# From the fourth group on, every engine works in written order: attention steps placed by hand among the feed-forward units, and the last weight blocks made inside that group

## The chip, the core and the metric

The kernel runs on one core of a Trainium2 chip. Its time is the device time of one execution in microseconds, as the median of repeated executions. Five engines work side by side, each through its own queue of instructions in order, and wait for one another through semaphores: TensorE (PE in the profile, its weight loads PEld), VectorE (DVE), ScalarE (ACT), GpSimd (POOL) and SyncE (SP, which here only issues DMAs). An instruction that waits holds up all that stands behind it on its engine, and nothing on the others, until they need its result.

## What is computed

Block attention over 8 batches, 8 heads and 576 positions in chunks of 64, and behind it a feed-forward layer with `h - tanh(h)` between its two matrices:

```python
scores = scale * np.matmul(q_c, k_c.transpose(0, 1, 2, 4, 3))   # 64 x 64 within a chunk
scores = scores - np.max(scores, axis=-1, keepdims=True)
attn = np.exp(scores)
attn = attn / (np.sum(attn, axis=-1, keepdims=True) + 1e-09)
out = np.matmul(attn, v_c)
x = out.transpose(0, 2, 1, 3).reshape(B * S, H * D)             # 4608 x 512
h = x @ w_in                                                    # w_in 512 x 2048
g = h - np.tanh(h)
return (g @ w_out).astype(np.float32)                           # w_out 2048 x 512
```

## The kernel before

**Groups.** The 4608 rows are worked through in nine groups of 512 (`SIZES`, four tiles of 128 rows). The attention of a group runs ahead of its feed-forward, in two halves `b` of two tiles each. Numbers are kept as a high and a low part (`xh`, `xl` and so on), and a product takes three matmul passes: high by high, high by low, low by high.

**The three first groups** (0 to 2) use `FeedForward`. In group 1 the first matrix is converted to half precision (`Half.convert`). In group 2 `Half.combine(j)` and `Half.shorten(j)`, for j = 0 to 7, make sums of blocks of the second matrix for a fast product: `combine` is six additions on POOL (L434 to L441), `shorten` four ACT scalings and four DVE subtractions (L454, L455) that leave `fast_w[j]`.

**From the fourth group on** (3 to 8, `FAST = 3`) `Fast` computes a product of the second matrix with seven instead of eight block products. A group has 16 units: (b, j), two halves of eight. For unit s, `Fast.run` issues:
- `gemm1(s)`: 24 matmuls on PE into `ph` (L576), of which there are two buffers;
- `shrink(s)`: tanh on ACT (L583), `ph - tanh` on DVE into u, which the profile calls `xl` (L584), and three sums on POOL (L585 to L587); u has two buffers;
- `split(s-1)`: high part on ACT (L596), low part on DVE (L597), of the unit before;
- `gemm2(s-3)`: 21 matmuls into `po` (L614), three units late. At the turn from one half to the next it pauses for one unit, so that two `gemm1` stand back to back and then two `gemm2`; `finish` (L629 to L640: 2 ACT, 6 DVE and 2 POOL instructions, 2 DMAs) empties `po` after unit 7 and unit 15.

**The attention of the next group** (`Late`) is laid between the units by `interleaved`: `sums` (largest values of q and k on ACT, L107, and of v on DVE, L124, then a maximum over partitions on POOL, L114, and small DVE instructions), `split` of q, k and v (ACT L297, DVE L298), `scores` (96 small matmuls, L308), `exponents`, `normalise`, `transpose` (to half precision, then two DMA transposes on SP, L348) and `values` (96 matmuls, then L360 and L361). `load` issues the DMAs of the group after that.

**What sets the order.** The text is only a wish: from the bar in `PLAN` on, a scheduler places instructions on every engine by the rank of their text and its own estimate of when operands are ready. So steps of a later group can be pulled ahead, on each engine by itself. What the scheduler has chosen is fixed before the kernel runs; on the chip each queue is worked in order.

Two things limit how far attention can be pulled apart: the tile `a` exists once and holds the split k, then the exponentials on their way to the DMA transposes, and, in this kernel, also the throwaway output of `sums` (L107); and `psa` in PSUM exists once for scores and values.

## Time and profile before

| What | us |
|---|---|
| median of 3 runs (lowest, highest) | 944.98 (944.39, 945.45) |
| the profiled execution's own time | 946.89 |
| its span, first to last instruction | 944.3 |
| busy in the span: PE, DVE, ACT, POOL | 849.3, 611.3, 473.3, 263.3 |

The mean granted TensorE clock of that execution was 0.965. In the trace, group 3 begins with its first `gemm1` at 339.76 us and group 8, the last, at 852.69. A row of the timeline reads: start, length, engine, line, operation, output<-inputs, shape, count, and in brackets how long the engine stood idle before it and what it waited for. "Busy" adds up instruction lengths; matmuls overlap their neighbours, so that a row of 24 matmuls is some 0.16 us longer than the step from its start to the start of the next row.

### The profile page before, as it was taken

The numbers are of one execution on the slowest core, as the hardware profiler recorded it, in microseconds if no ns is written. First come the engines' busy times: TensorE is split into PE (matmuls) and PEld (weight loads), VectorE is DVE, ScalarE is ACT, GpSimd is POOL, SyncE is SP. The second block draws the span as 40 slices with busy tenths as digits, with TensorE's granted clock in tenths as the row PEclk, the third lists the DMA queues.
The fourth block names the chain that finished last, engine by engine and source line by source line (L and its number), as shares of the span: only waits on it lengthen the run. The fifth ranks groups of instructions, "written<-read, shape, count | busy, mean of one in ns | idle before, by whom it ended". The sixth has DMA issues, their size and how long they took to land.

```text
span 944.3 us, 19977 instructions
## 1 busy us (share of the span) xinstructions
PE 849.3 (90%) x8525; PEld 700.0 (74%) x8525; DVE 611.3 (65%) x878; ACT 473.3 (50%) x767; POOL 263.3 (28%) x375
## 2 busy tenths in 40 slices
PE   9999999999998869897988888978979888889997
PEld 7888778887565558776876777767867777768886
DVE  6987987777787776465656466565746565555343
ACT  7797967656454744435434444336343534433342
POOL 0000000000266364242332242342323252334342
PEclk9999999999999969998999999999999899989999
DMA  9763534212220220303021122112131101010000
GB/s 257 220 192 138 175 100 140 52 46 70 88 51 19 26 108 24 69 24 90 24 68 47 24 68 68 46 40 74 47 49 43 24 24 24 12 36 24 1 23 23
DMA packets 61400, 63.14 MB, mean 67 GB/s; under 512 B 32640, under 2 KB 40832, under 8 KB 61312
## 3 DMA queue, kind: packets, MB, share of 16 engines
q1 hardware_dynamic: 61312, 61.88, 22.6%
q8 instruction: 66, 1.08, 0.5%
q14 instruction: 22, 0.18, 0.1%
HBM read 45.09 MB, written 9.44 MB: 58 GB/s over the span
## 4 chain that ended last, share of the span: by engine, by line
PE 32%; DVE 25%; POOL 14%; ACT 12%; issue 8%; DMA 7%; SPq 2%; ACTq 0%; DVEq 0%; POOLq 0%
PE ph L495 10%; PE po L519 9%; PE ph L576 6%; PE po L614 5%; POOL xl L587 4%; DVE xl L584 4%; DMA s<-a 4%; POOL xl L585 4%; ACT wh L596 4%; ACT gh L596 3%; DVE gl L597 3%; POOL xl L586 3%; DVE wh L597 2%; DVE wh L298 2%; DVE a L298 1%
## 5 line engine op out<-in xcount | busy, mean ns | idle before, releaser
L576 PE MATMUL ph<-xh,wl 128*128 128x256 f16 x2160 | 271.3, 286 | 45.5 <-DVE xl L584 45.3
L576 PEld LDWEIGHTS <-wl 128*128 128x128 f16 x2160 | 220.3, 102 | 84.1 <-issue 49.5
L585 POOL TENSOR_TENSOR xl<-xl 128x256 f32<-128x256 f32 x96 | 70.3, 733 | 357.0 <-DVE xl L584 293.2
L597 DVE SCALAR_TENSOR_TENSOR gl<-xl,to_g,gh 128x896 f16<-128x896 f32 x48 | 55.3, 1152 | 131.6 <-ACT gh L596 131.6
L596 ACT ACTIVATE gh<-xl,to_g 128x896 f16<-128x896 f32 x48 | 50.0, 1041 | 145.2 <-POOL xl L587 134.7
L597 DVE SCALAR_TENSOR_TENSOR wh<-xl,to_g,wh 128x896 f16<-128x896 f32 x48 | 59.1, 1231 | 80.3 <-ACT wh L596 80.2
L596 ACT ACTIVATE wh<-xl,to_g 128x896 f16<-128x896 f32 x48 | 50.0, 1042 | 119.7 <-POOL xl L587 119.7
L614 PEld LDWEIGHTS <-wh 128*128 128x128 f16 x1008 | 98.6, 98 | 11.4
L614 PE MATMUL po<-wl,wh 128*128 128x256 f16 x576 | 91.6, 273 | 0.0
L519 PE MATMUL po<-wh,gh 128*128 128x512 f32 x192 | 79.9, 416 | 4.4 <-ACT gh L510 4.4
L495 PE MATMUL ph<-xh,wl 128*128 128x512 f16 (+2 forms) x324 | 77.0, 375 | 4.0 <-DVE t L504 3.0
L614 PE MATMUL po<-wh,wh 128*128 128x256 f16 x432 | 78.5, 273 | 0.0
L519 PE MATMUL po<-wh,gl 128*128 128x512 f32 x192 | 76.5, 403 | 1.8 <-DVE gl L511 1.8
L519 PE MATMUL po<-wl,gh 128*128 128x512 f32 x192 | 76.4, 398 | 0.0
L584 DVE SCALAR_TENSOR_TENSOR xl<-ph,sig,t 128x512 f32<-128x512 f32 x96 | 71.0, 740 | 7.7 <-ACT t L583 7.7
L614 PEld LDWEIGHTS <-gh 128*128 128x128 f16 x672 | 65.7, 98 | 12.9 <-issue 4.9
L587 POOL TENSOR_TENSOR xl<-xl 128x256 f32<-128x256 f32 x96 | 71.4, 744 | 0.0
L583 ACT ACTIVATE t<-ph,sig 128x512 f32<-128x512 f32 x96 | 64.6, 673 | 3.9 <-PE ph L576 3.6
L614 PE MATMUL po<-wh,gh 128*128 128x256 f16 x336 | 55.7, 274 | 3.9 <-DVE wh L627 3.9
L308 PEld LDWEIGHTS <-wh 64*64 64x64 f16 x2688 | 27.4, 112 | 34.1 <-issue 33.7
L614 PE MATMUL po<-wl,gh 128*128 128x256 f16 x336 | 52.4, 273 | 0.0
L511 DVE TENSOR_TENSOR gl<-t,gh 128x512 fp32r<-128x512 f32 (+1 forms) x52 | 38.5, 742 | 19.5 <-ACT gh L510 17.4
(146 smaller groups left out, 1449.8 us busy)
## 6 DMA issues: line engine op xcount, KB each, us to landing
raw<-w_in SPq DMA_DIRECT2D x16, 512.0 KB, 3.9
raw<-w_out SPq DMA_DIRECT2D x16, 512.0 KB, 5.2
out<-wh SPq DMA_DIRECT2D x32, 256.0 KB, 2.0
rawk<-kL SPq DMA_DIRECT2D x28, 256.0 KB, 3.0
rawv<-vL SPq DMA_DIRECT2D x28, 256.0 KB, 2.9
xl<-qL SPq DMA_DIRECT2D x28, 256.0 KB, 2.8
qbd<-qE SPq DMA_DIRECT2D x16, 128.0 KB, 4.9
k<-kE SPq DMA_DIRECT2D x8, 256.0 KB, 5.0
```

The lines of the kernel that those rows point to most:

```text
L298: nc.vector.scalar_tensor_tensor(out=hl[1], in0=raw, scalar=to, in1=hl[0], op0=ALU.mult, op1=ALU.subtract)
L495: nc.tensor.matmul(ph, lhsT=self.weight(fc, 0, a)[:, kc * P:(kc + 1) * P], rhs=x[b][:, kc, cols], start=(k == 0), stop=(k == 3 * KC - 1))
L511: nc.vector.tensor_sub(gl, t, gh)
L519: nc.tensor.matmul(self.po[t], lhsT=gg[a][:, ts], rhs=self.weight(fc, 1, b), start=(fc == 0 and i == 0), stop=(fc == FC - 1 and i == 2))
L576: nc.tensor.matmul(self.ph[:, 1 - f::2, :], lhsT=half_w[fc][:, w, kc * P:(kc + 1) * P], rhs=rhs, start=(k == 0), stop=(k == 3 * KC - 1))
L583: nc.scalar.activation(t, self.ph, AF.Tanh, scale=sig)
L584: nc.vector.scalar_tensor_tensor(out=u[:, :4], in0=self.ph, scalar=sig, in1=t, op0=ALU.mult, op1=ALU.subtract)
L585: nc.gpsimd.tensor_add(u[:, 4:6], u[:, 1:3], u[:, 0:4:3])
L587: nc.gpsimd.tensor_sub(u[:, 0:4:3], u[:, 0:2], u[:, 2:4])
L596: nc.scalar.activation(gh, u, AF.Copy, scale=powers[1])
L597: nc.vector.scalar_tensor_tensor(out=gl, in0=u, scalar=powers[1], in1=gh, op0=ALU.mult, op1=ALU.subtract)
L614: nc.tensor.matmul(place[m], lhsT=part[:, self.SUM[m]], rhs=w[m][:, o], start=first, stop=(j == FC // 2 - 1 and part is gl), skip_group_ch ...
```

## The change

From group 3 on the code is put under `tc.manual_schedule()`: every engine takes its instructions in the order of the text. `Fast.run` becomes one loop over the 96 units of groups 3 to 8. `interleaved` stays for groups 2 and 3; for groups 4 to 8 a new function `ahead` places each step of the next group's attention at a unit of the group before it, with the unit's number and its half (0: behind `split`, 1: behind `gemm2`). The steps are cut smaller: `sums` without its tail (`scales`), `exponents` into `shifted` and `exponent`, `normalise` into `totals` and `divided`. In this order half b = 0 has its splits in units 5 and 6, its scores in 6, its transposes in 10 and its values in 12; half b = 1 stands eight units later, so that its last steps fall into units 0 to 4 of its own group. The throwaway output of `sums` goes to a tile `t`, no longer to `a`. `combine(6)`, `combine(7)` and `shorten(5)` to `shorten(7)` move out of group 2: they come in units 0 to 6 of group 3.

```diff
@@ -39,6 +39,9 @@
 LAG = 2
 FAST = 3
 FAST_LAG = 2
+ON_TIME = 6
+LATE_COMBINE = {6: 1, 7: 7}
+LATE_SHORTEN = {5: 0, 6: 6, 7: 12}
 RAW = 3
 WS = 2
 EARLY_FC = 8
...
@@ -264,17 +267,25 @@
             for n, src in (("q", qL), ("k", kL), ("v", vL)):
                 nc.sync.dma_start(out=self.raw[n][:, i], in_=src[p - NE])
 
-        def sums(self, g, n):
+        def sums(self, g, n, other=None):
 
             d = self.st[f"g{g}"]
             if n == "q":
                 d["sums"] = self.pool.tile([P, 3], F32, name="sums", bufs=2)
             some = self.raw[n][:, :SIZES[g]]
+            if n != "v" and other is not None:
+                spread(other.bitcast(U8).rearrange("p (a n) -> p a n", n=H * CH), some, d["sums"][:, "qkv".index(n):"qkv".index(n) + 1])
+                return
             if n != "v":
                 junk = self.pool.tile([P, 4, H * CH], F16, name="a", bufs=1).bitcast(U8).rearrange("p a n -> p (a n)")[:, :MOST * H * CH // P].rearrange("p (a n) -> p a n", n=H * CH) if self.junk is None else self.junk
                 spread(junk, some, d["sums"][:, "qkv".index(n):"qkv".index(n) + 1])
                 return
             largest(some.rearrange("p i n -> p (i n)"), d["sums"][:, 2:3])
+            if other is None:
+                self.scales(g)
+
+        def scales(self, g):
+            d = self.st[f"g{g}"]
             d["to"], d["from"] = (self.pool.tile([P, 3], F32, name=m, bufs=2) for m in ("to", "from"))
             power(self.pool, "x", d["sums"], d["to"], d["from"])
             d["exp"] = self.pool.tile([P, 1], F32, name="exp", bufs=2)
...
@@ -314,22 +325,37 @@
             self.products(lambda c, e, hp: ps[:, c, e, hp], lambda a, r, e, hp, u: q[a][r, e, hp, u], lambda b, r, e, hp, u: k[b][r, e, hp, u])
 
         def exponents(self, g, b):
+            self.shifted(g, b)
+            self.exponent(g, b)
+
+        def shifted(self, g, b):
             d = self.st[g, b]
             s = d["s"] = self.pool.tile([P, 2, 4, 2, CH], F32, name="s", bufs=1)
             mx = self.pool.tile([P, 2, 8, 1], F32, name="mx", bufs=2)
             ps = d["ps"].rearrange("p c e hp k -> p c (e hp) k")
             nc.vector.reduce_max(out=mx[:, :, :, 0], in_=ps, axis=AX.X)
             nc.vector.tensor_sub(s.rearrange("p e hp c k -> p c (e hp) k"), ps, mx.broadcast_to([P, 2, 8, CH]))
-            nc.scalar.activation(s, s, AF.Exp, scale=d["exp"])
+
+        def exponent(self, g, b):
+            d = self.st[g, b]
+            nc.scalar.activation(d["s"], d["s"], AF.Exp, scale=d["exp"])
 
         def normalise(self, g, b):
+            self.totals(g, b)
+            self.divided(g, b)
+
+        def totals(self, g, b):
             d = self.st[g, b]
             s = d["s"].rearrange("p e hp c k -> p (e hp c) k")
-            sm = self.pool.tile([P, 16, 1], F32, name="sm", bufs=2)
+            sm = d["sm"] = self.pool.tile([P, 16, 1], F32, name="sm", bufs=2)
             nc.vector.reduce_sum(out=sm[:, :, 0], in_=s, axis=AX.X)
             nc.vector.tensor_scalar_add(sm, sm, 1e-9)
             nc.vector.reciprocal(out=sm, in_=sm)
             nc.vector.tensor_scalar_mul(sm, sm, 2.0 ** 14)
+
+        def divided(self, g, b):
+            d = self.st[g, b]
+            s, sm = d["s"].rearrange("p e hp c k -> p (e hp c) k"), d["sm"]
             nc.vector.tensor_mul(s, s, sm.broadcast_to([P, 16, CH]))
 
         def transpose(self, g, b):
...
@@ -639,11 +661,13 @@
             for t, o in enumerate((oa, ob)):
                 nc.sync.dma_start(out=out[row + t * P:row + (t + 1) * P, :], in_=o)
 
-        def run(self, g, x, at):
-            self.group(g, x)
-            waited = False
-            for s in range(2 * FC // 2):
-                unit = divmod(s, FC // 2)
+        def run(self, at):
+            waited, n = False, 2 * FC // 2
+            for s in range((NG - FAST) * n):
+                if s % n == 0:
+                    g = FAST + s // n
+                    self.x, self.powers, self.row = xs[g], powers[g], FIRST[g] * P
+                unit = divmod(s % n, FC // 2)
                 self.gemm1(*unit)
                 before, self.ready = self.ready, None
                 self.shrink(*unit)
...
@@ -662,14 +686,37 @@
                             self.gemm2()
                 for f in at.pop(2 * s + 1, []):
                     f()
-            for k in sorted(at):
-                for f in at[k]:
-                    f()
-
-        def drain(self):
+            assert not at, at
             self.split()
             while self.queue:
                 self.gemm2()
+
+    def ahead(att, at, g):
+
+        o = 2 * FC * (g - 1 - FAST)
+
+        def put(unit, half, f, *args):
+            at[o + 2 * unit + half].append(lambda: f(*args))
+
+        for unit, n in (1, "q"), (2, "k"), (3, "v"):
+            put(unit, 0, lambda n=n: att.sums(g, n, ffn.tile([P, MOST], F32, name="t", bufs=3)))
+        put(4, 0, att.scales, g)
+        put(4, 1, lambda: powers.update({g: half.power_of(g)}))
+        put(5, 0, lambda: xs.update({g: new_half_x()}))
+        for b, u in enumerate((5, 13)):
+            put(u, 0, att.split, g, b, "q")
+            put(u, 1, att.split, g, b, "k")
+            put(u + 1, 0, att.split, g, b, "v")
+            if g + 1 < NG:
+                for i in (2 * b, 2 * b + 1):
+                    put(u + 1, 1, att.load, FIRST[g + 1] + i, i)
+            put(u + 1, 1, att.scores, g, b)
+            put(u + 2, 0, att.shifted, g, b)
+            put(u + 3, 0, att.exponent, g, b)
+            put(u + 3, 1, att.totals, g, b)
+            put(u + 4, 0, att.divided, g, b)
+            put(u + 5, 0, att.transpose, g, b)
+            put(u + 7, 0, lambda b=b: att.values(g, b, xs[g]))
 
 
     x, nx = new_x(), new_x()
...
@@ -755,10 +802,11 @@
     early_psum.close()
     ps_a = ctx.enter_context(tc.tile_pool(name="ps_l", bufs=1, space=PSUM, side="right", reuse_waits="tile"))
     late = ctx.enter_context(tc.tile_pool(name="att", bufs=1, side="right", reuse_waits="tile"))
-    att, half, over = Late(late), Half(late), defaultdict(list)
-    for g in range(1, NG):
-        x, nx = nx, new_half_x() if g + 1 < NG else None
-        at = interleaved(att, g + 1, nx) if nx else {}
+    att, half = Late(late), Half(late)
+    xs, powers, late_at = {}, {}, defaultdict(list)
+    for g in range(1, FAST):
+        x, nx = nx, new_half_x()
+        at = interleaved(att, g + 1, nx)
         if g == 1:
             half.powers()
             first_place = late.tile([P, DM], F32, name="first_place", bufs=1).bitcast(F16)
...
@@ -781,23 +829,20 @@
         if g < FAST:
             if g == FAST - 1:
                 for j in range(FC // 2):
-                    at[4 * j + 7].append(lambda j=j: half.combine(j))
-                    k = 4 * j + 9
-                    (at if k < 2 * (FC + LAG) else over)[k].append(lambda j=j: half.shorten(j))
+                    (at if j < ON_TIME else late_at)[4 * j + 7 if j < ON_TIME else LATE_COMBINE[j]].append(lambda j=j: half.combine(j))
+                    (at if j < ON_TIME - 1 else late_at)[4 * j + 9 if j < ON_TIME - 1 else LATE_SHORTEN[j]].append(lambda j=j: half.shorten(j))
             order = range(FC) if g < FAST - 1 else [j + f * FC // 2 for j in range(FC // 2) for f in range(2)]
             ff = FeedForward(g, x)
             ff.room(ps_o1, range(2))
             ff.room(ps_o2, range(2, SIZES[g]))
             ff.run([(fc, 0, SIZES[g]) for fc in order], at)
-            continue
-        if g == FAST:
-            for fs in over.values():
-                for f in fs:
-                    f()
-            post.extend(place_of(*n, F32) for n in half.free[:3])
-            fast = Fast((ps_o1, ps_o2))
-        fast.run(g, x, at)
-    fast.drain()
+    fast = Fast((ps_o1, ps_o2))
+    xs[FAST], powers[FAST] = nx, half.power_of(FAST)
+    for g in range(FAST + 1, NG):
+        ahead(att, late_at, g)
+    late_at[17].append(lambda: post.extend(place_of(*n, F32) for n in half.free[:3]))
+    with tc.manual_schedule():
+        fast.run(late_at)
 
 
 def kernel(**inputs):
```

**ACT, end of group 2.** Names: L503 is the tanh of a `FeedForward` unit, L510 the high part of it, L360 the values of group 3's second half, L297 the splits of q, k and v (`xl`, `rawk`, `rawv`) for group 4, L454 a step of `shorten`, L544 the copy of group 2's result. Before:

```order
L107 ACTIVATE a,sums<-xl 128x2048
L503 ACTIVATE t<-ph,sig 128x512
L107 ACTIVATE a,sums<-rawk 128x2048
L510 CAST gh<-t 128x512
L454 ACTIVATE wl_3693<-wh_3550,to_w 128x512
L454 ACTIVATE wl_3695<-wh_3555,to_w 128x512
L503 ACTIVATE t<-ph,sig 128x512
L510 CAST gh<-t 128x512
L360 ACTIVATE xh<-psa 128x4x128
L297 ACTIVATE wh_1696<-xl,to 128x1024
L297 ACTIVATE a<-rawk,to 128x1024
L503 ACTIVATE t<-ph,sig 128x512
```

The same place after the change (L529 is the tanh, L536 the high part, L386 the values, L570 the copy):

```order
L529 ACTIVATE t<-ph,sig 128x512
L536 CAST gh<-t 128x512
L529 ACTIVATE t<-ph,sig 128x512
L536 CAST gh<-t 128x512
L386 ACTIVATE xh<-psa 128x4x128 x2
L529 ACTIVATE t<-ph,sig 128x512
L536 CAST gh<-t 128x512
L570 COPY wh_2604<-po_2643 128x512
L570 COPY wh_2606<-po_2645 128x512
```

Group 4's sums and splits and the steps of `shorten(5)` have left the tail of group 2; only the values of group 3 still stand ahead of the last tanh.

**POOL, start of group 3.** L607 to L609 (before: L585 to L587) are the three sums of a unit, L460 to L467 (before: L434 to L441) a `combine`. After the change:

```order
L607 TENSOR_TENSOR xl<-xl 128x256
L608 TENSOR_TENSOR xl<-xl 128x128
L609 TENSOR_TENSOR xl<-xl 128x2x128
L460 TENSOR_TENSOR wh_3816<-wh_96,wl_97 128x512
L462 TENSOR_TENSOR wh_3818<-wh_1002,wl_1003 128x512
L464 TENSOR_TENSOR wl_3820<-wh_3818,wh_3816 128x512
L465 TENSOR_TENSOR wh_3821<-wh_3816 128x256
L466 TENSOR_TENSOR wh_3821<-wh_3818 128x256
L467 TENSOR_TENSOR wh_3816<-wh_3816,wh_3818 128x256
L607 TENSOR_TENSOR xl<-xl 128x256
```

Before, both last `combine` stood ahead of the first unit's sums; now the sums of unit 0 come first, then `combine(6)`, and the sums of unit 1 stand behind it.

**DVE, a middle group.** L298 (after: L309) is the low part of a split, L361 (L387) that of the values, L584 (L606) u of a unit, L597 (L619) the low part of a unit. Before, group 6's second half and group 7's first splits:

```order
L298 SCALAR_TENSOR_TENSOR wh_1697<-xl,to,wh_1696 128x1024
L298 SCALAR_TENSOR_TENSOR a<-rawk,to,a 128x1024
L361 SCALAR_TENSOR_TENSOR xh<-psa,xh 128x4x128
L298 SCALAR_TENSOR_TENSOR wh_1699<-rawv,to,wh_1698 128x1024
L361 SCALAR_TENSOR_TENSOR xh<-psa,xh 128x4x128
L584 SCALAR_TENSOR_TENSOR xl<-ph,sig,t 128x512
```

After the change, units 5 and 6 of a group:

```order
L606 SCALAR_TENSOR_TENSOR xl<-ph,sig,t 128x512
L619 SCALAR_TENSOR_TENSOR gl<-xl,to_g,gh 128x896
L309 SCALAR_TENSOR_TENSOR wh_1697<-xl,to,wh_1696 128x1024
L309 SCALAR_TENSOR_TENSOR a<-rawk,to,a 128x1024
L606 SCALAR_TENSOR_TENSOR xl<-ph,sig,t 128x512
L619 SCALAR_TENSOR_TENSOR gl<-xl,to_g,gh 128x896
L309 SCALAR_TENSOR_TENSOR wh_1699<-rawv,to,wh_1698 128x1024
L606 SCALAR_TENSOR_TENSOR xl<-ph,sig,t 128x512
```

Where five attention instructions stood in one run ahead of a unit's u, at most two stand there now, and each unit's own two instructions come between.

More of the change, by code (lines that the diff above doesn't have):

```diff
@@ L562, in __init__ @@
             self.g = [[t[:, :7 * P].rearrange("p (s n) -> p s n", n=P) for t in tiles[2 * i:2 * i + 2]] for i in range(FAST_LAG + 2)]
-        def group(self, g, x):
-            self.x, self.powers = x, half.power_of(g)
-            self.row = FIRST[g] * P
         def gemm1(self, b, j):
```

## The prediction

> **What bounds the kernel now.** I read the page's first lines, then a table of busy times by stretch, then the chain of waits, then the rows around one stall. A difference of up to 0.2% (about 1.9 us) is taken as what a measurement of this kernel cannot tell from no change.
>
> The span, then stretches of the span; columns are length, busy time and count of PE, weight loads, DVE, ACT and POOL, granted clock, DMA share, GB/s:
>
> ```profile
> span 944.3 us, 19977 instructions
> 339.76:439.95 100.19, 84.76 (x1043) 71.67 (x1042) 55.49 (x69) 41.01 (x52) 37.42 (x51) 0.91 0.17 43
> 542.55:645.52 102.97, 87.43 (x1106) 75.51 (x1104) 62.11 (x82) 44.15 (x54) 33.27 (x53) 0.97 0.18 52
> 852.69:944.30 91.61, 85.64 (x785) 76.51 (x782) 37.95 (x51) 31.48 (x39) 35.19 (x57) 0.99 0.05 18
> ```
>
> Groups 3 to 7, from the first `gemm1` of each to that of the next, take 512.93 us (339.76 to 852.69), 102.6 each. PE is the busiest engine in each stretch, yet it isn't full in one. The last group, which has no attention beside it, runs at a clock of 0.99. What a unit takes when nothing stops PE, the chain of waits shows in that group (start, length, engine):
>
> ```profile
> 279.00 2.80 PE po L519 x12
> ...
> 877.42 2.62 PE ph L576 x24
> 880.04 2.29 PE po L614 x21
> ...
> 929.16 8.64 PE po L614 x79
> ```
>
> A unit is 2.62 + 2.29 = 4.91 us, sixteen are 78.6, and the 96 units of groups 3 to 8 are 471.4. PE ends at 929.16 + 8.64 = 937.8, the span 6.5 later. So of the 604.5 us behind 339.76, 471.4 are units, 6.5 the tail, and some 20 are scores and values (below): about 106 are stalls of PE and a lowered clock. That sum is what the change can draw on. Its anatomy at one boundary, group 6 to 7 (timeline; the brackets hold the idle time ahead and what ended it):
>
> ```profile
> 632.90 1.22 DVE L340 TENSOR_TENSOR a<-s,a 128x1024 f16<-128x1024 f32 x1
> 637.43 0.57 PE L308 MATMUL psa<-s,wh 64*64 64x64 f16 x48 [4.22 <-DMA s<-a]
> 638.72 0.86 PE L308 MATMUL psa<-s,wh 64*64 64x64 f16 x48 [0.71 <-DMA s<-a]
> 638.82 1.91 ACT L107 ACTIVATE a<-xl 128x2048 uint8<-128x2048 f32 x1 [5.50 <-issue]
> 639.50 3.89 PE L576 MATMUL ph<-xh,wl 128*128 128x256 f16 x24
> 641.79 1.15 DVE L597 SCALAR_TENSOR_TENSOR gl<-xl,to_g,gh 128x896 f16<-128x896 f32 x1 [7.01 <-ACT gh L596]
> 652.30 2.78 PE L576 MATMUL ph<-xh,wl 128*128 128x256 f16 x24 [1.71 <-DVE xl L584]
> ```
>
> The reader is to see three things. Values stand on PE 4.22 and 0.71 us before the transposes of `a` land. L107 wants `a` as a place to throw its output away, and starts just as the transposes have read it: ACT, busy less than half the time, stands 5.5 us there, and the unit's `gh` behind it. DVE then waits 7.01 for `gh`, and PE, two `gemm1` on, 1.71 for DVE's u. And after PE has stood, a `gemm1` lasts 3.89 instead of 2.78: the clock falls.
>
> **The change part by part.** No PE, ACT or POOL instruction is added or taken out from group 3 on; they move. I rebuild the span from the places where PE stands.
>
> *Group 2's end.* Before (and with the late `combine` and `shorten`):
>
> ```profile
> 312.26 2.76 PE L495 MATMUL ph<-xh,wl 128*128 128x512 f16 x12
> 317.75 0.97 PE L308 MATMUL psa<-s,wh 64*64 64x64 f16 x96
> 320.21 2.75 PE L495 MATMUL ph<-xh,wl 128*128 128x512 f16 x12 [1.48 <-DVE t L504]
> 329.38 0.68 ACT L503 ACTIVATE t<-ph,sig 128x512 f32<-128x512 f32 x1
> 332.28 0.80 PE L519 MATMUL po<-wh,gh 128*128 128x512 f32 x1 [3.69 <-ACT gh L510]
> ```
>
> The last tanh starts at 329.38, some 6 us after its `gemm1`, because group 4's sums and splits and `shorten(5)` stood ahead of it on ACT and DVE; these rows leave. Without waits: values end at 317.75 + 1.0, the last `gemm1` 2.4 later (its 2.75 less the overlap) at 321.1, and three `gemm2` of 2.8 give a start of group 3 at **329.5** instead of 339.76. This holds as long as the tanh comes within the first two `gemm2`, 5.6 us; it needs 1.
>
> *Start of group 3.* The moved weight blocks now come between the units, and POOL works them in order:
>
> ```profile
> 331.26 1.25 POOL L434 TENSOR_TENSOR wh<-wh,wl 128x512 f32<-128x512 f32 x1 [6.70 <-DVE a L298]
> 336.33 1.03 DVE L455 SCALAR_TENSOR_TENSOR wh<-wh,to_w,wh 128x256 f16<-128x256 f32 x1
> 337.91 1.18 POOL L441 TENSOR_TENSOR wh<-wh,wh 128x256 f32<-128x256 f32 x1
> 896.65 0.72 POOL L585 TENSOR_TENSOR xl<-xl 128x256 f32<-128x256 f32 x1 [3.00 <-DVE xl L584]
> 898.50 1.04 ACT L596 ACTIVATE gh<-xl,to_g 128x896 f16<-128x896 f32 x1 [2.94 <-POOL xl L587]
> 899.57 1.15 DVE L597 SCALAR_TENSOR_TENSOR gl<-xl,to_g,gh 128x896 f16<-128x896 f32 x1 [3.00 <-ACT gh L596]
> 900.64 0.75 DVE L584 SCALAR_TENSOR_TENSOR xl<-ph,sig,t 128x512 f32<-128x512 f32 x1
> ```
>
> A `combine` takes POOL 7.8 us (331.26 to 339.09), a unit's sums 1.9 (896.65 to the start of `gh`), a `shorten` DVE some 3.9 (four of 0.75 to 1.03). Counted from the start S: u(0) 4.1, POOL's sums of it 6.0, `combine(6)` to 13.8, the sums of unit 1 to 15.7, its `gh` 16.7; then, on ACT in order, k's largest values (1.9) and tanh(3) 19.5; u(3) 20.2; on DVE `shorten(6)` to 25.5, v's largest values to 27.9, u(4) 28.7. `combine(7)` ends at 29.9, unit 4's sums at 31.8, the maximum over partitions, its turn on POOL behind them, at 32.9, the scales and powers at 35, q's and k's low parts at 39.4. Scores stand on PE behind seven `gemm1` and four `gemm2`, 27.5 us if nothing holds it: it stands 11.9, and 1.2 more go to the clock (3.89 against 2.78 above). I take **13**. Bounds: 6, if `shorten(6)` finds DVE's idle moments and the maxima come early; 20, if the next units' sums are late too.
>
> *Scores and values.*
>
> ```profile
> 610.77 0.97 PE L308 MATMUL psa<-a,wh 64*64 64x64 f16 x96
> 611.68 2.79 PE L576 MATMUL ph<-xh,wl 128*128 128x256 f16 x24
> ```
>
> Scores cost 0.91 from start to start; ten times, 9.1. Values need their transposes: `a` was complete at 632.90 + 1.22, and the second half of the values began 4.6 us later, at 638.72. In the new order transposes are issued in unit 10 and 18, values follow behind the `gemm1` of the second unit after. DVE's division and low part end some 3.7 us after `gemm1`(10), the data is there 8.3 after it; PE comes after 2.29 + 2.62 + 2.62 = 7.5. So 0.8 of the former 4.9 stays: 0.57 + 0.57 + 0.86 = 2.0 each, **20** for ten. Bounds 1.1 (no wait) and 6.1 (the wait as before).
>
> *DVE in units 1 to 6.* This is the dense place. A unit's own two instructions are 1.15 + 0.75 = 1.9; with attention a group has 62.11 on DVE, of 78.6. In units 1 to 6 fall `finish` of the half before, sums of v, values, the scales and three low parts:
>
> ```profile
> 602.71 0.69 DVE L361 SCALAR_TENSOR_TENSOR xh<-psa,xh 128x512 f16<-128x512 f32 x1
> 606.27 2.29 DVE L124 TENSOR_REDUCE sums<-rawv 128x1 f32<-128x2048 f32 x1 [2.22 <-DMA rawv<-vL]
> 615.08 0.87 DVE L627 SCALAR_TENSOR_TENSOR wh<-po,undo_g,wh 128x256 f32<-128x256 f32 x2
> 644.92 0.16 DVE L118 TENSOR_SCALAR from<-xtop 128x3 f32<-128x3 f32 x1
> 646.72 1.28 DVE L298 SCALAR_TENSOR_TENSOR wh<-xl,to,wh 128x1024 f16<-128x1024 f32 x1 [1.17 <-ACT wh L297]
> ```
>
> An estimate from these rows: `finish` 2.8 (six instructions, the first two 0.87 together, the others near that), v 2.3, values 1.4, some fourteen small instructions of the scales 2.2, three low parts 3.8, together 12.5, beside 6 x 1.9 = 11.4 of the units: 24 of 29.5 us. PE stands for u only when it comes two `gemm1` late (there are two `ph`), a slack of about 5 us. The tighter date is the scores'. From the end of unit 2's `gemm1`, PE reaches them after 2.29 + 4 x 4.91 + 2.0 for the values = 23.9. DVE has by then to do the u and low parts of four units (7.6), `finish`, v, values, scales and two low parts: 18.9 by the same numbers, and 4 to 5 more for its waits (the tanh, the maximum over partitions, ACT's high parts): about 23.5. That is on the edge, and I take **2.0 a group, 10** for the attention of groups 4 to 8, with 0.4 and 6 as ends (0.4: one small instruction or two too late; 6: near the old wait of 7.01).
>
> *At nothing.* L107 now throws its output into `t`, which no transpose reads, and so the 5.50 and 7.01 above go. The loads on SP, six each in units 6 and 14, stand four units (20 us) ahead of the transposes in the same queue:
>
> ```profile
> rawk<-kL SPq DMA_DIRECT2D x28, 256.0 KB, 3.0
> ```
>
> Landed 3.0 us after its issue, even six in a row are over in 18, so four units hide them; without that cover the transposes land late and the 4.22 comes back.
>
> *Sum* of the span: 329.5 + 471.4 + 9.1 + 20 + 13 + 10 + 6.5 = **859.5**. The profiled execution's own time is 946.89, 2.6 above its span: 862.1. The median of the runs, 944.98, lies 1.9 below that execution: **860**.
>
> **A rule against it.** In the order of before, a unit's low part waits for POOL's sums of the same unit; now it stands directly behind the next unit's u, while POOL sums that u. The second and third row here show a place where the two meet already:
>
> ```profile
> 623.70 0.46 POOL L586 TENSOR_TENSOR xl<-xl 128x128 f32<-128x128 f32 x1
> 627.96 1.77 DVE L333 TENSOR_TENSOR s<-s,sm 128x1024 f32<-128x1024 f32 x1
> 628.61 1.44 POOL L586 TENSOR_TENSOR xl<-xl 128x128 f32<-128x128 f32 x1
> ```
>
> The division takes 1.77 (L340 at 632.90 shows 1.22 for the same size, 0.5 less), and POOL's sum beside it 1.44 instead of 0.46. The Trainium skill, "SBUF — State Buffer", section "SBUF: two separate sides", says that DVE and GpSimd share one pair of ports as an exclusive lock: a DVE instruction with two inputs in SBUF and a GpSimd instruction that reads it block each other for the whole instruction. These two rows agree, but do not show that it is always so.
>
> **Rivals.**
>
> *Stalls almost all go.* The start of group 3 costs 6 instead of 13 and DVE is late by 0.4 a group instead of 2.0: 7 + 8 less, **845**. For it: DVE's 24 of 29.5 and ACT's 44 of 79 leave room. Against: the chain through POOL at the start, each step of which has a row.
>
> *DVE and POOL hold each other up.* If each of 26 two-input instructions a group (16 low parts, 10 of the attention) loses the 0.5 of the row above, DVE gets 13 us more per group: 75 of 78.6. Then the dense units run late by 4 more in each of five groups: **880**. It decides when a group's DVE time passes about 70. The Trainium skill's rule points this way. For it: the two rows; against: in the last group, POOL and DVE work side by side at 35.19 and 37.95, and units keep to 4.91.
>
> *Slower.* Written order makes one engine's wait everyone's wait:
>
> ```profile
> DVE gl L597 <- ACT gh L596: 131.6, 44, 7.1
> DVE wh L597 <- ACT wh L596: 80.2, 46, 3.0
> ```
>
> DVE stood 211.8 us over 96 low parts for ACT's high part, 2.2 a unit. If that stays, because ACT's written order brings each high part behind an attention step, DVE needs 62 + 16 x 2.2 + 10 for the other waits = 107 a group: 329.5 + 5 x 107 + 94 = 958.5, **959**. It decides when DVE's waiting passes 41 us a group, the 103 of now less 62. Against it: the low part of a unit now comes behind the u of the next, 4.9 us after POOL could start, while sums and high part take 1.9 + 1.04.
>
> *It doesn't do what it says:* the moved weight blocks take back what the earlier start of group 3 gives. With 20 at its start the sum is 867, within my range: the move alone is then worth 10.3 less 20, a loss, and the other groups win.
>
> **How the numbers follow.** Forecast 860 (852 to 870, its own range), chance 0.55. Nearly no stalls, 845: 0.17. Held up by ports, 880: 0.20. Slower, 959: 0.06. Partial success that ends at 0.2%: 0.02. The range leaves out the last two and the ends of the others: 843 to 888, from 845 less 2 to 880 plus what a wait of 1.7 more in each of five groups adds. Faster by over 0.2% 0.92, same 0.02, slower 0.06.
>
> **What would show it.** In the changed profile: the first `gemm1` of group 3 near 329.5; then one stall of 6 to 20 us ahead of that group's first scores, released by DVE's low part; group lengths near 86; ten waits of about 0.8 ahead of values; no row of DVE waiting 7 us for `gh`; granted clock above 0.97 behind group 3. Low parts of 1.6 instead of 1.15, or POOL sums of 1.4, would speak for the ports. The prediction is wrong if PE's idle moments in groups 4 to 7 come regularly, once a unit, rather than at scores and values.

## The result, and the profile after

| | before | after |
|---|---|---|
| median, us (lowest to highest) | 945.22 (944.39 to 946.30) | 885.08 (881.58 to 887.62) |
| ratio, 95% interval | | 0.936 (0.933 to 0.939) |
| profiled execution: own time, span | 946.89, 944.3 | 881.58, 879.8 |
| busy PE, DVE, ACT, POOL | 849.3, 611.3, 473.3, 263.3 | 823.3, 638.4, 471.0, 350.4 |

The change gains 6.4%. The forecast was 860, with 852 to 870 as its own range and 843 to 888 as the whole one: sign and whole range held, the narrow one didn't, and the time is 25 us above the forecast. The profiled execution is the fastest of the four, 3.5 below the median, where that of before lay 1.9 above its own. The sums below, like those of the prediction, are made against the profiled execution: 881.6 where the working gave 862.1, so that 19.5 us are to be found in the trace (20.3 by the span).

A table of stretches of the span, from the first `gemm1` of a group to that of the next, groups 3 to 6 and 8 (length; busy time and count of PE, weight loads, DVE, ACT, POOL; granted clock, DMA share, GB/s):

```profile
329.49:425.70 96.21, 80.04 (x946) 68.95 (x946) 64.38 (x78) 46.11 (x60) 56.19 (x61) 0.93 0.17 50
425.70:515.55 89.85, 83.31 (x1106) 73.98 (x1104) 66.22 (x83) 44.36 (x54) 49.09 (x54) 1.00 0.23 60
515.55:607.24 91.69, 84.81 (x1106) 74.94 (x1104) 66.24 (x83) 44.36 (x54) 49.27 (x54) 0.98 0.23 59
607.24:696.03 88.79, 83.38 (x1106) 74.09 (x1104) 65.97 (x83) 44.35 (x54) 49.27 (x54) 1.00 0.22 61
...
785.07:879.80 94.73, 86.89 (x881) 77.47 (x878) 54.59 (x62) 33.26 (x43) 49.42 (x57) 0.99 0.08 23
```

Group 3 begins at 329.49. A middle group takes 89 to 92 us where it took 102.6 (the prediction looked for 86); 78.6 units, 1.8 scores and 2.3 values would be 82.7. DVE has 4 us more a group than before, POOL 16 more, and yet the groups are shorter by 11 to 14. What PE still waits for (engine, tile and line, releaser: us in all, times, longest):

```profile
PE psa L319 <- DMA s<-a: 16.3, 21, 1.9
PE psa L319 <- DVE a L309: 12.5, 5, 2.6
PE psa L319 <- ACT a L308: 6.8, 4, 5.4
PE ph L598 <- DVE xl L606: 6.6, 4, 4.8
```

L319 are the small matmuls of scores and values. The first row is the values', waiting for the transposes. The second and third are the first scores of each group. The last lies in the first units of group 3 alone, so that in groups 4 to 7 PE stands at scores and values and not once a unit. How the second row comes about, POOL, DVE and ACT show in units 4 and 5 of group 4 (timeline: start, length, engine, line; the bracket is the idle time ahead and what ended it):

```profile
453.25 0.72 POOL L609 TENSOR_TENSOR xl<-xl 128x256 f32<-128x256 f32 x1
459.77 0.38 POOL L117 PARTITION_ALL_REDUCE xtop<-sums  x1 [5.80 <-issue]
460.19 0.17 DVE L121 TENSOR_SCALAR from<-xtop 128x3 f32<-128x3 f32 x1 [5.94 <-POOL xtop L117]
460.81 1.15 ACT L308 ACTIVATE wh<-xl,to 128x1024 f16<-128x1024 f32 x1 [2.59 <-DVE to L123]
461.65 0.74 DVE L606 SCALAR_TENSOR_TENSOR xl<-ph,sig,t 128x512 f32<-128x512 f32 x1
465.90 0.94 PE L319 MATMUL psa<-a,wh 64*64 64x64 f16 x92 [2.04 <-DVE a L309]
467.58 0.71 POOL L607 TENSOR_TENSOR xl<-xl 128x256 f32<-128x256 f32 x1 [7.42 <-issue]
```

The maximum over partitions (L117) takes 0.38 us, but POOL stands 5.80 ahead of it with nothing to wait for, and 7.42 behind it, although the u that it is to sum was there at 462.4 (461.65 + 0.74). DVE stands 5.94 of that time; everything of the chain to the scores comes after.

The Trainium skill, "GPSIMD Engine Reference", section "2.1 Instruction dispatch", says that the first call of a freshly loaded kernel on GpSimd pays about 6 us without an instruction in the profile. The 5.80 here agrees in length. What the trace does show are instructions of POOL's queue, which don't count as busy, on the lines of the maximum (L117) and of the next sum (L607); shortest/median/longest in ns, first and last start:

```profile
L117 POOLq MODIFY_POOL_CONFIG  x2: 1/1/1, 454.2 to 454.2; - x2
L607 POOLq MODIFY_POOL_CONFIG  x10: 83/83/83, 368.9 to 730.7; - x10
```

The first line is of group 4 alone: two of them stand 5.6 us ahead of the maximum at 459.77. The second is of the whole run: two stand right behind the maximum in each of groups 3 to 7. So the time is paid in each group, on the way to the maximum and on the way back, and not only on a first call.

### The profile page after: what moved, and what is told of

Its sections match the earlier page's. It is cut to its first block, busy times and chain, and to the rows that moved or that the text cites. A ratio compares the mean times of both kernels' runs of the same rounds, so it can differ in the third digit from the quotient of the medians.

```text
span 879.8 us, 20041 instructions
## 1 busy us (share of the span) xinstructions
PE 823.3 (94%) x8525; PEld 688.0 (78%) x8525; DVE 638.4 (73%) x878; ACT 471.0 (54%) x767; POOL 350.4 (40%) x375
## 4 chain that ended last, share of the span: by engine, by line
PE 66%; DVE 12%; issue 7%; POOL 6%; ACT 4%; DMA 4%; SPq 1%; ACTq 0%; DVEq 0%; POOLq 0%
PE ph L598 19%; PE po L636 18%; PE ph L521 11%; PE po L545 11%; DMA s<-a 3%; PE psa L319 2%; PE psa L245 1%; PE psa L197 1%; POOL xl L607 1%; DVE xl L606 1%; DVE sums L127 1%; ACT t L110 1%; DVE gl L619 1%; SPq L374 1%; DVE a L309 1%
## 5 line engine op out<-in xcount | busy, mean ns | idle before, releaser
L598 PE MATMUL ph<-xh,wl 128*128 128x256 f16 x2160 | 252.7, 275 | 6.6 <-DVE xl L606 6.6
L598 PEld LDWEIGHTS <-wl 128*128 128x128 f16 x2160 | 212.1, 99 | 33.6 <-issue 7.3
L607 POOL TENSOR_TENSOR xl<-xl 128x256 f32<-128x256 f32 x96 | 99.6, 1037 | 218.6 <-DVE xl L606 211.2
L606 DVE SCALAR_TENSOR_TENSOR xl<-ph,sig,t 128x512 f32<-128x512 f32 x96 | 71.6, 746 | 66.2 <-ACT t L605 65.4
L609 POOL TENSOR_TENSOR xl<-xl 128x256 f32<-128x256 f32 x96 | 89.8, 936 | 0.0
L619 DVE SCALAR_TENSOR_TENSOR gl<-xl,to_g,gh 128x896 f16<-128x896 f32 x48 | 67.5, 1406 | 30.3 <-ACT gh L618 30.3
L608 POOL TENSOR_TENSOR xl<-xl 128x128 f32<-128x128 f32 x96 | 87.8, 915 | 0.0
L619 DVE SCALAR_TENSOR_TENSOR wh<-xl,to_g,wh 128x896 f16<-128x896 f32 x48 | 64.7, 1349 | 17.6 <-ACT wh L618 17.5
L319 PEld LDWEIGHTS <-wh 64*64 64x64 f16 x2688 | 27.5, 109 | 44.1 <-issue 38.8
```

The costliest lines, as they stand in the source:

```text
L319: nc.tensor.matmul(ps(c, e, hp)[u * D:(u + 1) * D], lhsT=stationary(a, r, e, hp, u), rhs=moving(b, r, e, hp, u), start=(i == 0), stop=(i = ...
L598: nc.tensor.matmul(self.ph[:, 1 - f::2, :], lhsT=half_w[fc][:, w, kc * P:(kc + 1) * P], rhs=rhs, start=(k == 0), stop=(k == 3 * KC - 1))
L606: nc.vector.scalar_tensor_tensor(out=u[:, :4], in0=self.ph, scalar=sig, in1=t, op0=ALU.mult, op1=ALU.subtract)
L607: nc.gpsimd.tensor_add(u[:, 4:6], u[:, 1:3], u[:, 0:4:3])
L608: nc.gpsimd.tensor_add(u[:, 6], u[:, 1], u[:, 2])
L609: nc.gpsimd.tensor_sub(u[:, 0:4:3], u[:, 0:2], u[:, 2:4])
```

## The experiments

All times are medians in us; each kernel was run beside the kernel before. Diffs are against the changed kernel unless said otherwise.

| Kernel | Time | Ratio to before (95%) |
|---|---|---|
| after | 885.08 | 0.936 (0.933 to 0.939) |
| maximum replaced by a copy | 860.13 | 0.910 (0.908 to 0.912) |
| maximum by two DMAs | 869.26 | 0.920 (0.919 to 0.921) |
| sums and scales one unit earlier | 919.34 | 0.973 (0.971 to 0.975) |
| values 4.6 us later | 888.23 | 0.940 (0.939 to 0.942) |
| low part ahead of u | 920.38 | 0.974 (0.973 to 0.976) |
| low part ahead of u, maximum by DMAs | 897.85 | 0.951 (0.949 to 0.952) |
| text of after, order by the scheduler | 943.31 | 0.999 (0.998 to 0.999) |
| text of before, written order | 895.63 | 0.949 (0.947 to 0.950) |
| sums' throwaway output in `a` | 917.18 | 0.971 (0.969 to 0.973) |
| weight blocks back in group 2 | 881.71 | 0.933 (0.931 to 0.935) |
| DMAs, sums early, values late | 852.82 | 0.903 (0.901 to 0.904) |
| the same, blocks back | 846.47 | 0.896 (0.894 to 0.898) |

**The maximum over partitions.**

```diff
-        nc.gpsimd.partition_all_reduce(top, sums, channels=P, reduce_op=bass_isa.ReduceOp.max)
+        if name == "x" and late_group():
+            nc.gpsimd.tensor_copy(top, sums)
```

> The changed kernel, but from group 4 on the maximum over partitions (one GpSimd instruction per group) is a plain copy of the per-partition values on GpSimd; so this kernel leaves that maximum out. Theory A (GpSimd stands about 5.9 us before and 5 us behind each such instruction, and DVE, then PE's scores, wait for it): the waits ahead of the first scores of groups 4 to 7 (2.0 to 3.2 us each, 11.3 in all) fall below 3 in all, the stall at the start of group 3 falls from some 20 to 13 or less; 885 becomes 864 to 870. Theory B (DVE is simply too full in units 1 to 6): the waits stay, the time falls by 4 us at most.

860.13, 25 us less. PE's waits of the copy's run (its lines are 8 higher, L327 is L319):

```profile
PE psa L327 <- DMA s<-a: 14.2, 21, 1.4
...
PE psa L327 <- DVE a L317: 2.1, 1, 2.1
```

Of 19.3 us ahead of scores 2.1 are left, all in group 3; the values' waits stay. Theory A holds and was still too small: the waits that are gone, 17.2 ahead of scores and 2.1 of the values, are 19.3 of the 24.6 us between the two profiled executions, and PE's busy time fell by 5.8. Behind 227 us, no `MODIFY_POOL_CONFIG` is left in this run's trace. That the gain is as large as the distance from the forecast is chance: the forecast had 10 us for DVE's lateness in it, and the values' waits, which it had too small, are still here. DVE isn't too full in units 1 to 6: with 648.9 us it is busier here than in the changed kernel, and on time.

**The same without leaving the maximum out.**

```diff
+            place = dram.tile([P, 3], F32, name="place")
+            nc.sync.dma_start(out=place, in_=d["sums"])
+            wide = other[:, :3 * P]
+            nc.sync.dma_start(out=wide, in_=place.rearrange("(o p) n -> o (p n)", o=1).broadcast_to([P, 3 * P]))
...
+        if fast_now and name == "x":
+            nc.vector.reduce_max(out=top, in_=fast_now.pop(0).rearrange("p (q n) -> p n q", n=n), axis=AX.X)
```

> The changed kernel with the partition maximum of groups 4 to 8 made without GpSimd: the 128 x 3 values go out to memory by one DMA and come back to all partitions by another, issued in unit 3, and DVE takes the maximum of 3 x 128 values in unit 4. Nothing is left out. Theory A (GpSimd's dead time around that instruction was the loss): as with the plain copy, 860 to 868, with no idle time of 5 us or more on GpSimd in unit 4. Theory B (two DMAs one behind the other take as long as the dead time, 6 us, and DVE stands for them): 875 to 885, DVE waiting 3 us or more for the DMA.

869.26, just outside A's 860 to 868. Group 4 in its timeline:

```profile
449.19 0.33 SPq L294 DMA_DIRECT2D place<-sums  x1
451.19 0.33 SPq L296 DMA_DIRECT2D t<-place  x1
455.20 0.67 DVE L121 TENSOR_REDUCE xtop<-t 128x3 f32<-128x384 f32 x1 [2.40 <-DMA t<-place]
```

From the first issue to DVE's maximum are 6.0 us, as long as POOL's dead time; but POOL goes on meanwhile, and DVE stands 2.40 instead of 5.94. PE waits 9.0 us ahead of scores (2.1 with the copy), 5.9 of them in group 3. Both theories have a part of it.

**Could the maximum just be made earlier?**

```diff
-        for unit, n in (1, "q"), (2, "k"), (3, "v"):
+        for unit, n in (0, "q"), (1, "k"), (2, "v"):
...
-        put(4, 0, att.scales, g)
+        put(3, 0, att.scales, g)
```

> The changed kernel with the sums of q, k and v and the scales one unit earlier (units 0 to 3 instead of 1 to 4), the partition maximum on GpSimd as it is. Theory A (its dead time was only too late for the scores in unit 6): the waits ahead of the first scores, 2.0 to 3.2 us a group, go, 868 to 876. Theory B (DVE stands 6 us in that unit wherever it lies, and then comes late with u or the values): within 4 us of 885.

Neither: 919.34, 34 us slower. In group 6 of this run:

```profile
661.21 0.17 DVE L121 TENSOR_SCALAR from<-xtop 128x3 f32<-128x3 f32 x1 [8.02 <-POOL xtop L117]
664.19 0.60 ACT L386 ACTIVATE xh<-psa 128x512 f16<-128x512 f32 x1 [7.77 <-DVE xh L387]
673.37 0.27 PE L319 MATMUL psa<-a,wh 64*64 64x64 f16 x4 [5.75 <-ACT a L308]
```

DVE's stand for the maximum now lies ahead of the copies of the values on DVE (L387); ACT's second copy (L386) waits 7.77 for those, and the splits behind it on ACT are later for the scores than they were. The wait had been moved ahead of work that another engine needs.

**The values.**

```diff
-            put(u + 7, 0, lambda b=b: att.values(g, b, xs[g]))
+            put(u + 7, 1, lambda b=b: att.values(g, b, xs[g]))
```

> The changed kernel with the values one half step later: behind the two gemm2 of their unit instead of ahead of them (4.6 us later on PE). Theory A (the values stand on PE only because the DMA transposes land 0.5 to 1.9 us late for each half): the twenty waits, 15.6 us in all, go, and nothing else is late, since the result is used four units on: 870 to 874. Theory B (what follows the values on ACT and DVE in units 4 to 6 is then late for the scores): the waits move to the scores, gain under 5 us.

888.23: theory B in its sign, and no gain at all. The values' waits went entirely, and the scores' waits grew. In group 4:

```profile
461.05 0.17 DVE L121 TENSOR_SCALAR from<-xtop 128x3 f32<-128x3 f32 x1 [7.97 <-POOL xtop L117]
462.31 0.60 ACT L386 ACTIVATE xh<-psa 128x512 f16<-128x512 f32 x1 [9.52 <-DVE xh L387]
466.54 0.27 PE L319 MATMUL psa<-a,wh 64*64 64x64 f16 x4 [4.48 <-ACT a L308]
```

It is the case of the early sums again: the scales, and DVE's stand for the maximum, had come ahead of the values' copies. So the two waits are coupled through the maximum, and with it out of the way both should go:

> The changed kernel with the partition maximum by two DMAs, the sums one unit earlier, and the values behind the two gemm2 of their unit. Theory A (with the maximum out of the way, later values no longer push the scores): both kinds of wait go in groups 4 to 8, 869 less 13 to 17, so 852 to 857. Theory B (the copies behind the values still hold up ACT ahead of the splits, as they did with the values late alone): 863 or more.

852.82, as theory A said: 16.4 less than with the DMAs alone, no wait of the values left, and 0.6 us ahead of the first scores in each of groups 4 to 7. The scales stay in unit 4 here. What the early sums and the late values bring each by itself, with the DMAs, wasn't tried.

**Which part of the change gains: the written order, or the small steps?** First the text of after under the scheduler (the block `with tc.manual_schedule()` taken off around `fast.run`), then the text of before in written order (the same block put around its `fast.run` and `drain`).

> The changed kernel without the written order: the same text, steps and places, but from the fourth group on the scheduler orders the engines by its own estimates, as in the kernel before. Theory A (the gain is in the order that each engine works in; the scheduler again puts a unit's low part ahead of the next u, which alone cost 35 us): 910 to 935. Theory B (the gain is in the smaller steps and their places in the text): within 8 us of 885.

> The kernel before with nothing changed but that from the fourth group on every engine works in the order of the text, with the attention in its old large steps. Theory A (written order gains only because small steps were laid by hand): slower than 945, 950 to 1000, with PE waiting for DVE's u behind whole attention steps. Theory B (written order by itself brings most of the gain): 905 or less.

943.31 and 895.63: the small steps, the tile `t` and the moved blocks together gain 0.15% without the written order, and the written order alone gains 49 of the 60 us, with the old steps. The other 11 come only with the new steps in written order. What the order changes stands in DVE's waits for the high part, us in all and times; before had 211.8 (the two rows in the prediction). The scheduler's run:

```profile
DVE wh L619 <- ACT wh L618: 107.0, 44, 5.1
DVE gl L619 <- ACT gh L618: 106.9, 44, 3.0
```

The text of before in written order:

```profile
DVE gl L597 <- ACT gh L596: 19.8, 28, 1.9
...
DVE wh L597 <- ACT wh L596: 10.9, 27, 2.1
```

And after:

```profile
DVE gl L619 <- ACT gh L618: 30.3, 33, 5.5
...
DVE wh L619 <- ACT wh L618: 17.5, 22, 2.1
```

214 under the scheduler, 31 and 48 in written order. PE's waits for u go with them; before, the scheduler's run, and the text of before in written order (after: 6.6, above):

```profile
PE ph L576 <- DVE xl L584: 46.1, 32, 3.6
```

```profile
PE ph L598 <- DVE xl L606: 62.9, 35, 4.4
```

```profile
PE ph L576 <- DVE xl L584: 2.1, 2, 1.6
```

Both texts put a unit's low part behind the next u; the scheduler moves it ahead (by the order of DVE's rows, in 89 of 95 units of before and in 88 of its run here; in written order in none). To test that one place, `split` was put ahead of `shrink` in the changed kernel. This also puts ACT's high part ahead of the next tanh:

```diff
-                before, self.ready = self.ready, None
-                self.shrink(*unit)
-                before, self.ready = self.ready, before
                 self.split()
-                self.ready = before
+                self.shrink(*unit)
```

> The changed kernel with split(s-1) ahead of shrink(s) in each unit: DVE's low part stands ahead of u again, and no longer beside GpSimd's sums of that u. Theory A (the two block each other, but GpSimd is not on the path that PE waits for): the middle sum on GpSimd falls from a median of 1.30 us to 0.45, low parts from 1.57 to 1.15, busy GpSimd from 350 us to some 265 and DVE from 638 to some 610, while the time moves by 4 us at most. Theory B (the prediction's rival: DVE's time is what PE waits for): the time falls by 10 us or more with them. Theory C: the low part waits for ACT's high part ahead of u, u comes late, and the time rises by 5 us or more.

920.38: theory C, 35 us lost. Its DVE waits for the high part are back:

```profile
DVE gl L619 <- ACT gh L618: 99.4, 43, 6.7
DVE wh L619 <- ACT wh L618: 71.3, 41, 3.0
```

The loss could still have come from the dead time of the maximum, which DVE meets at once in this order. So the same with the maximum by DMAs:

> The low part ahead of u in each unit, and the partition maximum by two DMAs. Theory A (a loop of waits: with the low part ahead of u, each unit's u, GpSimd's sums 1.9, ACT's high part 1.04, the low part 1.15 and the next u 0.75 follow one another, 4.84 of the unit's 4.91 us, so that attention work on DVE has no room): the loss of 35 us against the low part behind u stays almost whole, 895 to 905 against the 869 of the same kernel with the low part behind u. Theory B (the loss came from GpSimd's dead time, which DVE met at once through the low part): 880 or less.

897.85, against 869.26 with the low part behind u: 28.6 of the 35.3 us stay. Theory A. The other 6.7 go with the maximum. Low part ahead of u is a loop through three engines, and the prediction's own rows show its length: from a POOL sum at 896.65 over the high part at 898.50 and the low part at 899.57 to the next u at 900.64, and 0.83 more to its POOL sum (as from the u before, at 895.82, to 896.65), 4.82 us, where a unit on PE takes 4.91. In the last group that just keeps up. That attention's work on the three engines lengthens it beyond PE's pace in the other groups is argued from these rows; the waits agree: against the kernel with the low part behind u, PE waits 14.7 for u instead of 6.6, and 23.9 for the transposes instead of 15.2. Behind u, the low part is out of the loop.

The ports. Two groups of instructions of the first of these two runs, and after them the same two of the changed kernel (shortest/median/longest in ns, first and last start):

```profile
L608 POOL TENSOR_TENSOR xl<-xl x96: 442/452/1441, 335.4 to 905.6; 128x128 f32<-128x128 f32 x96
...
L619 DVE SCALAR_TENSOR_TENSOR gl<-xl,to_g,gh x48: 1150/1152/1249, 338.6 to 898.2; 128x896 f16<-128x896 f32 x48
```

```profile
L608 POOL TENSOR_TENSOR xl<-xl x96: 443/1302/1436, 335.0 to 866.3; 128x128 f32<-128x128 f32 x96
...
L619 DVE SCALAR_TENSOR_TENSOR gl<-xl,to_g,gh x48: 1135/1572/1629, 338.1 to 860.8; 128x896 f16<-128x896 f32 x48
```

Beside one another, both are longer; apart, both are short, and the kernel is 35 us slower. By itself that doesn't show what they lose to each other, since the same edit brings the loop. But in groups 4 to 7 of the changed kernel PE never waits for u. It does wait for the values' transposes, and there a part is the ports'. In group 4:

```profile
487.96 1.75 DVE L366 TENSOR_TENSOR a<-s,a 128x1024 f16<-128x1024 f32 x1
493.65 0.57 PE L319 MATMUL psa<-s,wh 64*64 64x64 f16 x48 [1.82 <-DMA s<-a]
```

L366 completes `a`. It took 1.22 in before, with no sum of POOL beside it, so that 0.5 of this wait of 1.82 can be theirs. In the fastest kernel of the study (last in the table) low parts and sums are as long as here (medians 1.57 and 1.30), and PE waits 1.6 us in all for u and not at all for these transposes: what is lost there costs PE almost nothing.

**The throwaway output** of the sums of q and k goes to `a` again.

```diff
-            put(unit, 0, lambda n=n: att.sums(g, n, ffn.tile([P, MOST], F32, name="t", bufs=3)))
+            put(unit, 0, lambda n=n: att.sums(g, n, late.tile([P, 4, H * CH], F16, name="a", bufs=1).rearrange("p a n -> p (a n)")[:, :MOST * 2].bitcast(F32) if n != "v" else 1))
```

> The changed kernel with the throwaway output of the sums of q and k in the tile a again. In written order the sums of k then stand on ACT until the DMA transposes of the half before have read a. Theory A (this held up ACT and the chain in each group, as the prediction had it): ACT waits some 5 us in each of four to five groups, PE 1 to 3 of them: 890 to 900. Theory B (the partition maximum on GpSimd ends later anyway and covers it): within 3 us of 885.

917.18, 32 us lost where theory A expected 5 to 15. In group 6:

```profile
647.35 1.91 ACT L110 ACTIVATE a<-rawk 128x2048 uint8<-128x2048 f32 x1 [6.79 <-issue]
...
649.98 0.60 PE L636 MATMUL po<-wh,gh 128*128 128x256 f16 x4 [2.17 <-ACT wh L651]
```

ACT stands 6.79, by the order of the text for `a` (the row names no releaser, but it starts with the second half of the values, when both transposes have read `a`); behind it wait not only the chain to the scores but the copies that empty `po` (L651), and PE with them (8.4 us in four waits, of which neither kernel had one). It belongs to this order of steps: the text of before in written order has this output in `a`, too, and takes 895.63. What makes the difference there wasn't tried.

**The weight blocks.**

```diff
-ON_TIME = 6
-LATE_COMBINE = {6: 1, 7: 7}
-LATE_SHORTEN = {5: 0, 6: 6, 7: 12}
+ON_TIME = 8
+LATE_COMBINE = {}
+LATE_SHORTEN = {7: 0}
```

> The changed kernel with the last weight blocks made in group 2 again (combine(6), combine(7), shorten(5), shorten(6) there, shorten(7) in unit 0 of group 3). Theory A (the move was about worth what it cost): group 3 starts 4 to 10 us later, its stall ahead of the first scores shrinks from 20 to 8 to 14; time within 4 us of 885. Theory B (the move was the larger gain): 6 us or more slower. Theory C (the move is a loss): 5 us or more faster.

881.71, 3.4 less: theory A. Group 3 starts 5.6 later, at 335.14, and PE waits 6.9 us in it up to its first scores instead of 14.9. Still, the ranges of the runs (879.05 to 883.08 here, 881.58 to 887.62 after) overlap. With most other waits gone it can be told:

> The same, and the last weight blocks made in group 2 again. Theory A (the move of the blocks was a small loss, as it came out alone, -3): 2 to 6 us less than the kernel with the blocks late, 847 to 854. Theory B (with the maximum gone the moved blocks no longer disturb the start of group 3): the same or up to 4 us more.

846.47 (845.16 to 847.96) against 852.82 (852.08 to 853.09): 6.4 less, somewhat beyond theory A's 6. The move out of group 2 is a loss, and this kernel, complete in what it computes, is the fastest of the study: 10.4% below before.

## Why the prediction came near, and where it was off

Against the profiled execution, term by term (us):

| Term | Forecast | Measured |
|---|---|---|
| start of group 3 | 329.5 | 329.5 |
| units, scores, tail | 487.0 | 487.1 |
| values with their waits | 20 | 27.0 = 20 x 0.57 + 15.6 |
| stall at the start of group 3 | 13 | 20.3 = 96.2 - 71.7 - 1.8 - 2.4 |
| DVE late for the scores | 10 | 11.3 = 2.0 + 3.1 + 3.0 + 3.2 |
| the rest, spread over the groups | 0 | 4.6 |
| span | 859.5 | 879.8 |

(71.7 is 16 `gemm1` and 13 `gemm2` of group 3, 1.8 and 2.4 its scores and values. Units and scores are counted as in the forecast, 4.91 and 0.91 each; what they took beyond that is in the last row but one, which nothing here takes apart.)

- **Group 2's end** was right to a tenth of a microsecond, start and cause: the last tanh no longer waits. Only 5.6 of the 10.3 are the weight blocks', as the run with the blocks back shows; it keeps the rest without moving them.
- **The start of group 3** failed in one step of its chain: "the maximum over partitions, its turn on POOL behind them, at 32.9", 1.1 us behind POOL's sums. It took 6.3, from 362.65 to 368.92. The rows of it, and what the two waits then cost PE in clock:

```profile
359.95 4.19 PE L598 MATMUL ph<-xh,wl 128*128 128x256 f16 x24 [4.80 <-DVE xl L606]
361.93 0.72 POOL L609 TENSOR_TENSOR xl<-xl 128x256 f32<-128x256 f32 x1
368.54 0.38 POOL L117 PARTITION_ALL_REDUCE xtop<-sums  x1 [5.89 <-issue]
371.81 0.27 PE L319 MATMUL psa<-a,wh 64*64 64x64 f16 x4 [5.38 <-ACT a L308]
374.67 1.44 PE L319 MATMUL psa<-a,wh 64*64 64x64 f16 x92 [2.58 <-DVE a L309]
376.04 4.67 PE L598 MATMUL ph<-xh,wl 128*128 128x256 f16 x24
```

  5.2 us of the 7.3 that were missing are this step, 1.9 the second slow `gemm1` (4.67 instead of 2.78; only one was counted). With the copy in place of the maximum, 5.9 of the 8.0 us that PE waits ahead of these scores go.
- **This was to be seen in the trace of before.** There, too, POOL had nothing running on either side of the maximum. Ahead of it the profile names ACT as the releaser, since the sums of k came last, at 643.64. The pair of `MODIFY_POOL_CONFIG` stands at 636.87, 6.91 ahead of the maximum where after has 5.6 to 5.9, so the wait for ACT seems to have covered the other. Behind it stands a row that names none:

```profile
643.78 0.39 POOL L114 PARTITION_ALL_REDUCE xtop<-sums  x1 [7.11 <-ACT a L107]
650.92 0.71 POOL L585 TENSOR_TENSOR xl<-xl 128x256 f32<-128x256 f32 x1 [6.75 <-issue]
```

- **DVE in units 1 to 6**: the sum of 10 came near by luck. It counted five groups of 2.0, although group 3 had its stall in the row above already; four were measured, at 2.0 to 3.2. And the cause did not hold. The working counted DVE's load to 23.5 of 23.9 us and called it the edge; with the maximum as a copy the same load is on time. A number that comes out isn't a step that holds.
- **Values**: the second half's 0.8 was right (0.5 to 1.4 measured), but the first half waits as well (0.5 to 1.9), which the working left out. That they wait for nothing but the landing of the transposes, the late values show: from group 3 on not one wait is left there.
- **The anatomy of before** fell in its cause. It made the throwaway output in `a` the start of the chain that ends in DVE's 7.01. But the scheduler's run has that output in `t` and gains 0.15%. And the u that PE waits 1.71 for, at 651.50, stands on DVE right behind five attention instructions, from 646.72 on, and not behind that low part. What held before up was, by its rows, the loop over the low part; one edit shows the loop's price in the changed kernel, and in before itself the place wasn't changed alone. The prediction had the right rows, 211.8 us of DVE's waits for the high part, but only to price a rival, and the right argument, that the low part now comes behind the next u, only against that rival. In its sum the loop doesn't appear; that the sum came near is because it was built from the new order, in which the loop is gone.
- **The rivals.** "Held up by ports" named 880, and the time is near it, yet not for its reason. The rule of the Trainium skill on DVE's and GpSimd's shared ports ("SBUF — State Buffer", section "SBUF: two separate sides") agrees with the rows of both kernels. The sign that was named for it, low parts of 1.6 and sums of 1.4, came as well, but PE waits for little of it. The upper end of the range was worked out from this rival, so that the range held is in part luck. "Slower" had the right mechanism and much too high a price: DVE's waits for the high part were to cost 99 us more than the forecast; with the low part ahead of u, 170.7 of the 211.8 us of them are back, and they cost 35. The moved blocks were priced at a gain of 10.3 and a stall of 13 or more, a small loss: measured 3.4, and 6.4 where nothing else covers it.
- **The loads on SP**, costed at nothing, are named by no wait of PE. Whether they delay a transpose wasn't tried.

## What to carry to other kernels

Look in a tuned kernel for a loop that goes once through several engines in each unit, and add up its rows against the unit's pace: here 4.82 against 4.91, so that the attention beside it slowed the kernel though no engine was full. An instruction that waits is worth placing by what stands behind it in its queue, not by when its result is wanted; moved a unit earlier, the same wait cost 34 us more. And where a row is released by "issue" after several idle microseconds, price that as part of the instruction ahead of it or behind it.

## What the hardware showed unexpectedly

- The maximum over partitions costs POOL 5.8 to 6.0 us ahead of it and 4.5 to 5.2 more behind it (in group 4: operand ready at 462.4, sum started at 467.58) for 0.38 us of work, in each of groups 3 to 7, with a pair of `MODIFY_POOL_CONFIG` at the start of either.
- A GpSimd instruction that begins while DVE runs the low part ends about as if it had begun when that ended. In the changed kernel:

```profile
659.18 1.14 DVE L619 SCALAR_TENSOR_TENSOR wh<-xl,to_g,wh 128x896 f16<-128x896 f32 x1
659.34 1.56 POOL L607 TENSOR_TENSOR xl<-xl 128x256 f32<-128x256 f32 x1 [1.45 <-DVE xl L606]
```

  The sum takes 0.72 alone; here it ends at 660.90, 0.58 after the low part's recorded end at 660.32. POOL's busy time grew by 87 us with the change, and the kernel is 60 us faster.
